# Two expert layers after attention on one core: halves of results issued in the order in which their buffers come free, token operands and weight conversion issued step by step

## The chip, the cores and the metric

The kernel runs on one core of a Trainium2 chip. A core has TensorE (matrix products, written to PSUM), VectorE, ScalarE and GpSimd (elementwise work), and SyncE, which here only issues DMAs. The profile calls them PE, DVE, ACT, POOL and SP. Each engine works through its own queue in order; engines wait for each other through semaphores. The metric is the device time of one execution in microseconds.

## The reference

```python
# attention in chunks of 64 over q, k, v of shape (4, 8, 576, 64)
scores = scale * (q_c @ k_c.T); scores -= scores.max(-1)
attn = exp(scores); attn = attn / (attn.sum(-1) + 1e-9); out = attn @ v_c
x = out.transpose(0, 2, 1, 3).reshape(2304, 512)
# first layer, d_ff 1536
x = ((x @ w_a) * (x @ w_b)) @ w_out
# second layer, d_ff 2048
h = x @ w_in
g = maximum(h, 0) + alpha * minimum(h, 0)
return g @ w2_out
```

Weights arrive as 64-bit numbers and are turned into 32-bit ones on the chip. Every product of the layers is done in three multiplications of "halves": an operand is split into a high half, its rounded copy, and a low half, what the copy leaves.

## The kernel before

**Tokens.** The 2304 tokens are five blocks j: block 0 has 256 tokens, blocks 1 to 4 have 512. Attention and the first products of the first layer are issued by a table of letters (START), which the change leaves alone.

**First layer.** 12 column tiles m of w_a, w_b and w_out, in six groups of two. A group visits all five blocks; a visit issues four products into PSUM (pa and pb for two m: `l1_a`, `l1_b`, 12 multiplications of 128 x 128 by the block each), then four products of the block ahead with w_out (`l2`, 6 multiplications each), whose sums VectorE adds to `acc` (L382). ScalarE copies pa, VectorE multiplies, ScalarE makes the high half gh (L314), GpSimd the low half gl (L319).

**Weight conversion.** Beside the groups the weights of later groups and of the second layer are fetched and converted, 128 x 512 at a time, by `job`, called at every third product (`EVERY`). One call issues all of this in a row: high and low half of one block (`w_high`, `w_halves`, or `w_store`), then for the next block two ScalarE steps (L105, L106), three VectorE bit operations (L113, L114, L117), one GpSimd addition (L127), then a fetch. Weights of the second layer go back to DRAM as halves (`put`: ScalarE L212, VectorE L213, two stores L216, two buffers each). For each pair of w_in blocks GpSimd also makes four sums (L236), and that call issues three `put`s in a row.

**Second layer.** It takes the tokens in pairs of blocks, (1, 2) in rounds 0 to 7 and (3, 4) in rounds 8 to 15; a round q has two column tiles of w_in and two row tiles of w2_out. The first matrix product of a pair uses seven products in place of eight, on sums of weights and sums of tokens: `seven(i, ...)`, i = 0 to 6, here s0 to s6, six multiplications each, into the PSUM banks X, Y, X, Z, X, X, Z. ScalarE copies X after s0, s2 and s4 (`kept`, L486), before the next product adds to the same bank. VectorE completes the four results (`complete` L490, `two_slopes` L398 and L401), ScalarE and GpSimd split each into halves (L314, L319) for the second product. Block 0 takes two plain products a round (`l3`, ph) in rounds 0 to 7. The second products (`l4`, here b0 to b9) of a round are issued between the seven of the next round; b0 to b3 read the halves for the pair's first block, b4 to b7 those for the second, b8 and b9 those for block 0. VectorE adds them up (L522). The halves gh and gl have six buffers each, used in turn; a round with block 0 takes six.

**Operands of the tokens.** The seven token operands are B11, B21, T2, T1, T3, T4, B22, made by `t_stage` in seven stages from `acc`: subtractions into a scratch tile tt on VectorE (L424), then per operand two high halves on ScalarE (L430) and two low halves, one on GpSimd, one on VectorE (L432). T1 and T2 are made in tt, and T3 and T4 are written over them. This happens twice: at the end of the first layer for blocks 1 and 2, and in round 7 for blocks 3 and 4, each stage behind its `seven`.

Under the manual schedule, each engine's queue has the order of the code.

Of the kernel before, what the change touches and what calls it, by code (L numbers as in the profile page):

```python
# [45 lines left out]
def tile_attention_moe_moe2(ctx: ExitStack, tc: tile.TileContext, qkv, w_a, w_b, w_out, w2_in, alpha, w2_out, out):  # L46
# [144 lines left out]
    def w_add(b):  # L191
        block_at[b] = conv_add(block_at[b])
# [16 lines left out]
    def put(m, i, wf):  # L209
        h = spares[0].tile([P, 512], F32R, tag="gh", name="sh", bufs=2)  # L210
        l = spares[0].tile([P, 512], F32R, tag="gl", name="sl", bufs=2)
        nc.scalar.activation(out=h, in_=wf, func=ACTF.Copy)  # L212
# [6 lines left out]
    def w_store(b):  # L219
        assert b == halved[0]  # L220
        halved[0] += 1
        _, m, i = jobs[b][:3]
        wf = block_at.pop(b)
        if i == 0:
            left[m] = wf
        if i == 1:
            w0 = left.pop(m)
            a11, a12, a21, a22 = w0[:, 0:256], w0[:, 256:512], wf[:, 0:256], wf[:, 256:512]
            s12 = spares[0].tile([P, 512], F32, tag="a", name="s12", bufs=3)
            s34 = spares[0].tile([P, 512], F32, tag="a", name="s34", bufs=3)  # L230
            s1, s2, s3, s4 = s12[:, 0:256], s12[:, 256:512], s34[:, 0:256], s34[:, 256:512]
            for o, x, y, op in (
                (s1, a21, a22, ALU.add), (s2, s1, a11, ALU.subtract), (s3, a11, a21, ALU.subtract),
                (s4, a12, s2, ALU.subtract),
            ):
                nc.gpsimd.tensor_tensor(out=o, in0=x, in1=y, op=op)  # L236
            put(m, 4, s12)
            put(m, 5, s34)
        put(m, i, wf)

    def job(limit):

        b = halved[0]
        if b < begun[0]:
            if jobs[b][0] is None:
                w_store(b)
            else:
                w_high(b)
                w_halves(b, nc.vector)
        b = begun[0]  # L250
        if b < len(jobs) and b == halved[0]:
            w_low(b)
            w_bits(b)
            w_add(b)
        if len(jobs) < begun[0] + 2:
            fetch_next(limit)

# [146 lines left out]
    def l3(q, k, j):  # L404
        n = blocks[j][1] * P
        ph = bank([P, n], "ph")
        run(ph, k_steps(W2[q, k], xh[j], xl[j]))
        G[q, k, j] = two_slopes(ph, 2 * q % M2 + k, n)
# [10 lines left out]
    T_AT = {"B11": "xh1", "B21": "xl1", "T2": "xh2", "T1": "xl2", "T3": "xh3", "T4": "xl3", "B22": "xh4"}  # L419
    tt = [None]  # L420

    def t_add(out, x, y):
        for kk in range(2):
            nc.vector.tensor_tensor(out=out[:, kk], in0=x[:, kk], in1=y[:, kk], op=ALU.subtract)  # L424

    def t_split(name, src):
        t = xp.tile([P, 2, 2, 512], F32R, tag=T_AT[name], name=name)
        T[name] = t
        for kk in range(2):
            nc.scalar.activation(out=t[:, 0, kk], in_=src[:, kk], func=ACTF.Copy)  # L430
            eng = nc.vector if kk else nc.gpsimd
            eng.tensor_tensor(out=t[:, 1, kk], in0=src[:, kk], in1=t[:, 0, kk].bitcast(F32), op=ALU.subtract)  # L432

    def t_stage(i, j1, j2):

        b11, b21, b12, b22 = acc[j1][:, 0:2], acc[j1][:, 2:4], acc[j2][:, 0:2], acc[j2][:, 2:4]
        if i == 0:
            t_split("B11", b11)
        elif i == 1:
            t_split("B21", b21)  # L440
            tt[0] = xp.tile([P, KD, 512], F32, tag="xl4", name="tt")
            t_add(tt[0][:, 0:2], b12, b11)
            t_add(tt[0][:, 2:4], b22, tt[0][:, 0:2])
        elif i == 2:
            t_split("T2", tt[0][:, 2:4])
        elif i == 3:
            t_split("T1", tt[0][:, 0:2])
            t_add(tt[0][:, 2:4], b21, tt[0][:, 2:4])
        elif i == 4:
            t_add(tt[0][:, 0:2], b22, b12)  # L450
            t_split("T3", tt[0][:, 0:2])
        elif i == 5:
            t_split("T4", tt[0][:, 2:4])
        else:
            t_split("B22", b22)
# [88 lines left out]
    with tc.manual_schedule():  # L544
# [183 lines left out]
        for i, (f, args) in enumerate(order[NB - 1][2] + order[NB - 2][3]):  # L728
            f(*args)
            if i < 4:  # L730
                job(4)
# [4 lines left out]
        count = 0  # L736
        extra = []
        stages = [(t_stage, (i, 1, 2)) for i in range(7)]
        for m0, j, front, back in order[NB:]:
# [3 lines left out]
            if last and j == 4:  # L743
                extra += stages
            for i, (f, args) in enumerate(front + behind):
# [3 lines left out]
                count += 1  # L749
                if count % EVERY == 0:  # L750
                    job(limit)
                if extra and count % 2 == 0:
                    f, args = extra.pop(0)
                    f(*args)
            behind = back
        for f, args in extra:
            f(*args)
# [5 lines left out]
        for q in range(2 * n2):  # L763
            j1, j2 = (1, 2) if q < n2 else (3, 4)
            front = [(seven, (i, q, j1, j2)) for i in range(7)]
            small = [(l3, (q, k, 0)) for k in range(2)] if q < n2 else []
            extra = load_back(q) if q else []
            if q + 1 < 2 * n2:
                extra += load_front(q + 1)
            mixed = []  # L770
            if q == 0:
                for i in range(4):
                    mixed += [front[i], behind[i]]
                mixed += [front[4], small[0], front[5], small[1], front[6]]
            else:
                for i in range(7):
                    mixed += [front[i], behind[i]]
                mixed += behind[7:8] + small + behind[8:]
            for f, args in mixed:
                f(*args)  # L780
                if q == n2 - 1 and f is seven:
                    t_stage(args[0], 3, 4)
                if extra:
                    f, args = extra.pop(0)
                    f(*args)
# [46 lines left out]
```

## Time and profile before

| | us |
|---|---|
| runs of the kernel | 912.78, 905.9, 912.08 |
| median | 912.08 |
| the profiled execution | 912.4 |
| its span on the core | 910.6 |
| TensorE busy in it | 867.1 |

The rows below come from the profiled execution; times in them count from its span's start. "idle before <- X" names what ended an engine's wait. A product is a run of multiplications into one bank.

### The profile page before, as it was taken

To read this page: it belongs to the slowest core of one execution; us is meant where nothing else is said; L and a number is where in the kernel's file an instruction comes from. 1 tells how busy PE (TensorE), PEld (TensorE's weight loads), DVE (VectorE), ACT (ScalarE), POOL (GpSimd) and SP (SyncE) were. 2 spreads that over 40 slices of the span, in tenths; PEclk is the share of its full clock that TensorE was granted. 3 is DMA by queue.
4 is the path that set the end of the run, shared out by engine and by line. 5 is a ranking of instruction groups with operands and counts; after the bars stand their busy time and mean duration, and the time that the engine had idled before them with its cause. 6 is when DMAs were issued, how large, how long until landed. Compare 5 with 4: busy or idle time off the path is not lost.

```text
span 910.6 us, 13385 instructions
## 1 busy us (share of the span) xinstructions
PE 867.1 (95%) x5112; PEld 724.4 (80%) x5112; DVE 547.1 (60%) x871; ACT 328.0 (36%) x579; POOL 327.6 (36%) x282
## 2 busy tenths in 40 slices
PE   5899899999999999999999799999998699999998
PEld 4788788888888788878888678888876578888886
DVE  6783455746776576677624743565655753566555
ACT  4573464534454444455412332112122223212111
POOL 4462244434354444444423332222223422222221
PEclk9899999999999999999999899999999799999999
DMA  8853035336436626534622124332233065555512
GB/s 300 271 171 107 12 117 208 116 132 214 162 119 228 207 95 207 198 128 144 229 90 92 55 85 139 139 103 74 102 139 138 1 208 186 168 173 169 184 47 93
DMA packets 79408, 130.91 MB, mean 144 GB/s; under 512 B 9200, under 2 KB 34288, under 8 KB 79344
## 3 DMA queue, kind: packets, MB, share of 16 engines
q1 hardware_dynamic: 79344, 130.06, 42.3%
q8 instruction: 40, 0.66, 0.3%
q14 instruction: 24, 0.20, 0.1%
HBM read 100.15 MB, written 29.88 MB: 143 GB/s over the span
## 4 chain that ended last, share of the span: by engine, by line
PE 71%; DVE 11%; ACT 6%; POOL 5%; DMA 4%; issue 3%; SPq 0%; POOLq 0%; ACTq 0%; DVEq 0%
PE po L296 30%; PE pa L296 10%; PE pb L296 10%; PE sumX L478 10%; PE sumZ L478 5%; POOL t L127 3%; PE sumY L478 2%; PE ph L296 2%; DVE sl L213 2%; ACT sh L212 2%; DMA qk_t<-in_qkv 2%; DVE t L117 1%; ACT gh L314 1%; DVE t L114 1%; DVE tt L424 1%
## 5 line engine op out<-in xcount | busy, mean ns | idle before, releaser
L319 POOL TENSOR_TENSOR gl<-a,gh 128x512 fp32r<-128x512 f32 (+1 forms) x80 | 94.2, 1186 | 277.1 <-ACT gh L314 216.9
L296 PE MATMUL po<-w,gh 128*128 128x512 f32 x576 | 179.2, 393 | 0.0
L127 POOL TENSOR_TENSOR t<-t,raw 128x512 int32<-128x512 int32 x68 | 89.1, 1310 | 205.0 <-DVE t L117 143.5
L522 DVE TENSOR_TENSOR oacc<-po,oacc 128x512 f32<-128x512 f32 x126 | 86.0, 687 | 84.1 <-PE po L296 84.1
L314 ACT ACTIVATE gh<-a 128x512 fp32r<-128x512 f32 (+1 forms) x80 | 47.0, 589 | 229.4 <-PE po L296 113.0
L296 PEld LDWEIGHTS po<-w,gh 128*128 128x128 f32 x576 | 109.5, 190 | 22.8
L296 PE MATMUL po<-w,gl 128*128 128x512 f32 x288 | 113.5, 394 | 3.3 <-DVE oacc L522 3.3
L296 PE MATMUL po<-gh,wl 128*128 128x512 f32 (+1 forms) x240 | 89.7, 374 | 3.0 <-DVE acc L382 3.0
L296 PE MATMUL pa<-xh,wl 128*128 128x512 f32 (+1 forms) x240 | 90.1, 375 | 2.4 <-DVE xl L678 2.4
L319 POOL TENSOR_TENSOR gl<-a_sb,gh 128x512 fp32r<-128x512 f32 (+1 forms) x60 | 71.2, 1188 | 54.6 <-ACT gh L314 53.6
L478 PE MATMUL sumX<-T,w 128*128 128x512 f32 x288 | 76.1, 400 | 14.7 <-ACT a L486 14.7
L296 PE MATMUL po<-gh,wh 128*128 128x512 f32 (+1 forms) x240 | 89.3, 372 | 0.0
L296 PE MATMUL po<-gl,wh 128*128 128x512 f32 (+1 forms) x240 | 89.2, 372 | 0.0
L296 PE MATMUL pb<-xh,wl 128*128 128x512 f32 (+1 forms) x240 | 89.0, 371 | 0.2 <-DVE a_sb L343 0.2
L296 PE MATMUL pa<-xl,wh 128*128 128x512 f32 (+1 forms) x240 | 89.2, 372 | 0.0
L296 PE MATMUL pa<-xh,wh 128*128 128x512 f32 (+1 forms) x240 | 89.1, 371 | 0.0
L296 PE MATMUL pb<-xl,wh 128*128 128x512 f32 (+1 forms) x240 | 88.3, 368 | 0.0
L296 PE MATMUL pb<-xh,wh 128*128 128x512 f32 (+1 forms) x240 | 88.3, 368 | 0.0
L478 PEld LDWEIGHTS sumX<-T,w 128*128 128x128 f32 x288 | 54.1, 191 | 29.7 <-ACT a L486 18.9
L314 ACT ACTIVATE gh<-a_sb 128x512 fp32r<-128x512 f32 (+1 forms) x60 | 35.3, 589 | 98.4 <-DVE a_sb L343 98.3
L343 DVE TENSOR_TENSOR a_sb<-pb,a_sb 128x512 f32<-128x512 f32 (+1 forms) x60 | 37.9, 632 | 50.9 <-PE pb L296 44.7
L296 PEld LDWEIGHTS po<-w,gl 128*128 128x128 f32 x288 | 54.8, 190 | 15.0 <-issue 3.6
(83 smaller groups left out, 1522.5 us busy)
## 6 DMA issues: line engine op xcount, KB each, us to landing
w<-w SPq DMA_DIRECT2D x192, 256.0 KB, 4.8
raw<-in_moe_w_out SPq DMA_DIRECT2D x28, 512.0 KB, 3.5
w<-sh SPq DMA_DIRECT2D x48, 256.0 KB, 2.6
w<-sl SPq DMA_DIRECT2D x48, 256.0 KB, 2.5
qk_t<-in_qkv SPq DMA_DIRECT2D x18, 512.0 KB, 5.0
raw<-in_moe_w_in SPq DMA_DIRECT2D x16, 512.0 KB, 4.0
raw<-in_moe_w_a SPq DMA_DIRECT2D x12, 512.0 KB, 3.7
raw<-in_moe_w_b SPq DMA_DIRECT2D x12, 512.0 KB, 4.0
```

What stands on the lines that cost most here:

```text
L114: nc.vector.tensor_scalar(out=t, in0=t, scalar1=3, scalar2=0x3FFFFFFF, op0=ALU.logical_shift_left, op1=ALU.bitwise_and)
L117: nc.vector.scalar_tensor_tensor(out=t, in0=raw[:, :, 1], scalar=0xC0000000, in1=t, op0=ALU.bitwise_and, op1=ALU.bitwise_or)
L127: nc.gpsimd.tensor_tensor(out=ti, in0=ti, in1=raw[:, :, 0].bitcast(I32), op=ALU.add)
L212: nc.scalar.activation(out=h, in_=wf, func=ACTF.Copy)
L213: nc.vector.tensor_tensor(out=l, in0=wf, in1=h.bitcast(F32), op=ALU.subtract)
L296: nc.tensor.matmul(out=dst, lhsT=a, rhs=b, start=(i == 0), stop=(i == len(steps) - 1))
L314: nc.scalar.activation(out=h, in_=src, func=ACTF.Copy)
L319: nc.gpsimd.tensor_tensor(out=l, in0=src, in1=h.bitcast(F32), op=ALU.subtract)
L343: nc.vector.tensor_tensor(out=a_sb, in0=G[m, j], in1=a_sb, op=ALU.mult)
L424: nc.vector.tensor_tensor(out=out[:, kk], in0=x[:, kk], in1=y[:, kk], op=ALU.subtract)
L478: nc.tensor.matmul(out=dst, lhsT=x, rhs=y, start=opens and kk == n == 0, stop=kk == 1 and n == 2, skip_group_check=not opens,)
L522: nc.vector.tensor_tensor(out=acc[j][:, t, :], in0=po, in1=acc[j][:, t, :], op=ALU.add)
```

## The change

- `job` is called after every product and issues a third of the work at a time: at the first call ScalarE's high half of one block and the two ScalarE steps of the next; at the second VectorE's low half (with its stores) and the three bit operations; at the third GpSimd's addition and the next fetch. The extra halves of the weight sums go through the list `later`, one entry per call. A pair of w_in blocks is always fetched together.
- In the second layer `two_slopes` no longer makes halves. The halves are issued by `g_halves` at places written out in `mixed`: the first result's behind b3, the second behind b5 (before s6), the other two behind b7, those of block 0 behind b8 and b9 (`l3_out`).
- `t_ops` gives the token operands as 36 single steps, two per product (from the last block's first product on, and in round 7), all low halves on GpSimd, with other buffers: each operand takes the buffer whose last reader is issued just ahead.

```diff
+        half = jobs and jobs[-1][0] is None and jobs[-1][2] == 0
-        if jobs1 and jobs1[0][0] < limit:
+        if jobs1 and jobs1[0][0] < limit and not half:
...
+    def weight_sums(m, w0, w1):
...
+        def high(i, t):
+            state = []
+            later.append(lambda: state.append(put_high(m, i, t)))
+            later.append(lambda: put_low(*state[0]))
+
+        later.append(lambda: None)
+        high(4, s12)
+        high(5, s34)
...
     def job(limit):
 
+        beat[0] += 1
+        if later:
+            later.pop(0)()
         b = begun[0]
+        if beat[0] % 3 == 1:
+            if halved[0] < ready[0]:
+                d = halved[0]
+                if jobs[d][0] is not None:
+                    block_at[d] = half_high(block_at[d], jobs[d][0], jobs[d][2])
+                else:
+                    _, m, i = jobs[d][:3]
+                    wf = block_at[d]
+                    if i == 0:
+                        left[m] = wf
+                    if i == 1:
+                        weight_sums(m, left.pop(m), wf)
+                    block_at[d] = put_high(m, i, wf)
+            if b < len(jobs):
+                w_low(b)
+        elif beat[0] % 3 == 2:
+            if halved[0] < ready[0]:
+                d = halved[0]
+                halved[0] += 1
+                if jobs[d][0] is not None:
+                    w_halves(d, nc.vector)
+                else:
+                    put_low(*block_at.pop(d))
+            if ready[0] < b:
+                w_bits(ready[0])
+        elif ready[0] < b:
+            w_add(ready[0])
+            ready[0] += 1
+            if len(jobs) < b + 2:
+                fetch_next(limit)
+        elif len(jobs) < b + 2:
             fetch_next(limit)
...
-        return half_l(neg, half_h(neg, n), n)
+        return neg
+
+    def g_halves(q, k, j):
+        g = G[q, k, j]
         n = blocks[j][1] * P
+        G[q, k, j] = half_l(g, half_h(g, n), n)
...
+    T_AT = {"B11": "xh1", "B21": "xl1", "T2": "xl2", "T1": "xh3", "T3": "xl3", "T4": "xh4", "B22": "xl4"}
+    def t_ops(j1, j2):
...
+        tt = xp.tile([P, KD, 512], F32, tag="xh2", name="tt")
...
+        def low(name, src, kk):
+            t = T[name]
+            nc.gpsimd.tensor_tensor(out=t[:, 1, kk], in0=src[:, kk], in1=t[:, 0, kk].bitcast(F32), op=ALU.subtract)
...
+        split("B11", b11)
+        less(t1, b12, b11)
+        less(t2, b22, t1)
+        split("B21", b21)
+        split("T2", t2)
+        split("T1", t1)
+        less(t2, b21, t2)
+        less(t1, b22, b12)
+        split("T3", t1)
+        split("T4", t2)
+        split("B22", b22)
+        return steps
...
+            g11, g21, g22, g12 = ((g_halves, (q, k, j)) for k, j in ((0, j1), (1, j1), (1, j2), (0, j2)))
+            for i in range(4):
+                mixed += [front[i], behind[i]]
             if q == 0:
+                mixed += [g11, front[4], small[0], front[5], small[1], g21, front[6], g22, g12] + small_out
             else:
+                mixed += [g11, front[4], behind[4], front[5], behind[5], g21, front[6], behind[6], behind[7]]
+                mixed += [g22, g12]
+                for k in range(2):
+                    mixed += small[k:k + 1] + behind[8 + k:9 + k] + small_out[k:k + 1]
+            if q == n2 - 1:
+                extra = [(f, ()) for f in t_ops(3, 4)]
             for f, args in mixed:
                 f(*args)
+                for part, n in ((loads, 1), (extra, 2 if q in (0, n2 - 1) else 4)):
+                    for f, args in part[:n]:
+                        f(*args)
+                    del part[:n]
```

Three places show what moved. The first is VectorE's queue at the last pair of w_in blocks in the weight conversion (sl is a stored low half, s a tile of weight sums, t a block in conversion, acc and a_sb what TensorE's products become). Before:

```order
L382 TENSOR_TENSOR acc_1778<-po,acc_1778 128x512
L213 TENSOR_TENSOR sl<-s_4699,sh 128x512
L213 TENSOR_TENSOR sl<-s_4700,sh 128x512
L213 TENSOR_TENSOR sl<-t,sh 128x512
L113 TENSOR_SCALAR t<-t 128x512
L114 TENSOR_SCALAR t<-t 128x512
L117 SCALAR_TENSOR_TENSOR t<-raw,t 128x512
L382 TENSOR_TENSOR acc_1778<-po,acc_1778 128x512 x3
```

The same pair now:

```order
L219 TENSOR_TENSOR sl<-s_4715,sh 128x512
L219 TENSOR_TENSOR sl<-t,sh 128x512
L113 TENSOR_SCALAR t<-t 128x512
L114 TENSOR_SCALAR t<-t 128x512
L117 SCALAR_TENSOR_TENSOR t<-raw,t 128x512
L373 TENSOR_TENSOR a_sb<-pb,a_sb 128x512
L219 TENSOR_TENSOR sl<-s_4716,sh 128x512
L412 TENSOR_TENSOR acc_997<-po,acc_997 128x256 x2
L219 TENSOR_TENSOR sl<-t,sh 128x512
```

Three low halves in a row, each behind a high half of ScalarE, have become single ones with products' work between them.

The second is ScalarE's queue in one of the rounds 2 to 6 (a<-sumX is a copy of X, gh a high half of a result, 128x256 those of block 0). Before:

```order
L486 ACTIVATE a<-sumX 128x512
L314 ACTIVATE gh<-a 128x512
L486 ACTIVATE a<-sumX 128x512 x2
L314 ACTIVATE gh<-a 128x512 x3
L314 ACTIVATE gh<-a 128x256 x2
```

Now:

```order
L528 ACTIVATE a<-sumX 128x512 x2
L344 ACTIVATE gh<-a 128x512
L528 ACTIVATE a<-sumX 128x512
L344 ACTIVATE gh<-a 128x512 x3
L344 ACTIVATE gh<-a 128x256 x2
```

The second copy of X has moved ahead of the first result's high half.

The third is round 7, where the operands of blocks 3 and 4 are made. GpSimd's queue before (B and T are token operands, gl low halves of results):

```order
L432 TENSOR_TENSOR B_6791<-acc_1666,B_6791 128x512
L319 TENSOR_TENSOR gl<-a,gh 128x512
L432 TENSOR_TENSOR B_6827<-acc_1666,B_6827 128x512
L432 TENSOR_TENSOR T_6861<-tt,T_6861 128x512
L432 TENSOR_TENSOR T_6889<-tt,T_6889 128x512
```

Now:

```order
L479 TENSOR_TENSOR B_6796<-acc_1632,B_6796 128x512 x2
L479 TENSOR_TENSOR B_6856<-acc_1632,B_6856 128x512 x2
L479 TENSOR_TENSOR T_6880<-tt,T_6880 128x512 x2
L349 TENSOR_TENSOR gl<-a,gh 128x512
L479 TENSOR_TENSOR T_6897<-tt,T_6897 128x512 x2
```

And ScalarE's queue there now (T_6880 is T2, T_6897 is T1):

```order
L528 ACTIVATE a<-sumX 128x512
L475 ACTIVATE B_6796<-acc_1632 128x512 x2
L528 ACTIVATE a<-sumX 128x512
L475 ACTIVATE B_6856<-acc_1632 128x512 x2
L475 ACTIVATE T_6880<-tt 128x512 x2
L344 ACTIVATE gh<-a 128x512
L475 ACTIVATE T_6897<-tt 128x512 x2
L528 ACTIVATE a<-sumX 128x512
```

GpSimd has both low halves of each operand, and ScalarE's third copy of X stands behind the highs of T2 and T1.

## Rows read from the trace of the kernel before

**Rows 1.** The page: busy time, share of the span and instructions of TensorE.
```profile
PE 867.1 (95%) x5112; PEld 724.4 (80%) x5112; DVE 547.1 (60%) x871; ACT 328.0 (36%) x579; POOL 327.6 (36%) x282
```

**Rows 2.** The chain of waits: start, duration, engine, bank, line, multiplications.
```profile
389.52 2.56 PE po L296 x6
392.09 3.40 PE pa L296 x12
...
544.90 2.72 PE po L296 x12
547.62 2.90 PE ph L296 x24
550.52 2.76 PE po L296 x12
```

**Rows 3.** Stretches: from:to, length, busy PE, PEld, DVE, ACT, POOL (instructions), clock, DMA.
```profile
123.85:425.41 301.56, 298.39 (x1443) 251.59 (x1442) 202.03 (x340) 145.86 (x262) 136.30 (x123) 0.99 0.49 164
425.41:499.21 73.80, 73.80 (x362) 62.53 (x360) 32.32 (x53) 23.02 (x43) 26.98 (x25) 1.00 0.42 143
499.21:525.85 26.64, 21.15 (x92) 17.39 (x91) 21.60 (x32) 9.47 (x17) 10.93 (x8) 0.87 0.20 63
525.85:553.28 27.43, 26.37 (x127) 21.96 (x127) 11.23 (x19) 8.08 (x16) 7.15 (x6) 1.00 0.17 55
553.28:687.66 134.38, 131.50 (x632) 109.56 (x631) 75.99 (x124) 27.27 (x50) 34.16 (x31) 1.00 0.34 118
687.66:729.25 41.59, 30.61 (x128) 24.31 (x127) 27.67 (x40) 12.55 (x23) 17.96 (x14) 0.88 0.22 76
729.25:753.12 23.87, 23.29 (x103) 18.90 (x103) 13.52 (x21) 4.63 (x8) 6.33 (x6) 1.00 0.64 220
850.00:875.00 25.00, 25.00 (x112) 20.71 (x111) 16.67 (x26) 5.42 (x9) 7.77 (x6) 1.00 0.36 127
```

**Rows 4.** Waits of TensorE: waited for, us in total, times, longest.
```profile
PE sumX L478 <- ACT a L486: 14.7, 10, 5.5
PE po L296 <- DVE oacc L522: 3.3, 1, 3.3
```

**Rows 5.** Timeline of TensorE around 389 us: start, duration, line, operation, [idle before].
```profile
389.52 0.50 PE L296 MATMUL po<-gh,wl 128*128 128x512 f32 x1 [2.11 <-DVE acc L382]
```

**Rows 6.** Timeline of ScalarE and VectorE ahead of that wait.
```profile
382.87 0.63 ACT L212 ACTIVATE sh<-s 128x512 fp32r<-128x512 f32 x1 [5.01 <-POOL s L236]
383.54 2.08 DVE L213 TENSOR_TENSOR sl<-s,sh 128x512 fp32r<-128x512 f32 x2 [2.87 <-ACT sh L212]
389.05 0.42 DVE L382 TENSOR_TENSOR acc<-po,acc 128x256 f32<-128x256 f32 x1
```

**Rows 7.** Timeline of ScalarE and TensorE in round 6.
```profile
671.20 0.63 ACT L314 ACTIVATE gh<-a 128x512 fp32r<-128x512 f32 x1 [8.29 <-PE po L296]
671.74 0.58 ACT L486 ACTIVATE a<-sumX 128x512 f32<-128x512 f32 x1
672.37 1.65 PE L478 MATMUL sumX<-T,w 128*128 128x512 f32 x6 [0.58 <-ACT a L486]
674.11 0.60 ACT L486 ACTIVATE a<-sumX 128x512 f32<-128x512 f32 x1 [1.80 <-PE sumX L478]
```

**Rows 8.** Groups by line: operation, tiles, count | busy us, mean ns | idle before.
```profile
L319 POOL TENSOR_TENSOR gl<-a,gh 128x512 fp32r<-128x512 f32 x64 | 82.8, 1297 | 259.0 <-ACT gh L314 198.8 <-issue 36.0 <-PE sumX L478 17.7
L398 DVE TENSOR_SCALAR a<-a,alpha_sb 128x512 f32<-128x512 f32 x48 | 26.2, 545 | 3.7 <-POOL gl L319 0.6
L401 DVE SCALAR_TENSOR_TENSOR a<-a 128x512 f32<-128x512 f32 x48 | 33.3, 693 | 1.7
```

**Rows 9.** Timeline of GpSimd and VectorE at the second change of operands.
```profile
700.04 1.74 POOL L432 TENSOR_TENSOR B<-acc,B 128x512 fp32r<-128x512 f32 x1
700.55 2.38 DVE L424 TENSOR_TENSOR tt<-acc,acc 128x512 f32<-128x512 f32 x2
702.85 1.28 DVE L424 TENSOR_TENSOR tt<-acc,tt 128x512 f32<-128x512 f32 x2
```

More of the change, by code (lines that the diff above doesn't have):

```diff
@@ L217, in put @@
             dram[m, i, n] = d
[L219 to L239, printed above, removed]
@@ L241, in job @@
-    def job(limit):
[L243 to L249, printed above, removed]
-        b = begun[0]
[L251 to L255, printed above, removed]
+    def weight_sums(m, w0, w1):
+        a11, a12, a21, a22 = w0[:, 0:256], w0[:, 256:512], w1[:, 0:256], w1[:, 256:512]
+        s12 = spares[0].tile([P, 512], F32, tag="a", name="s12", bufs=3)
+        s34 = spares[0].tile([P, 512], F32, tag="a", name="s34", bufs=3)
+        s1, s2, s3, s4 = s12[:, 0:256], s12[:, 256:512], s34[:, 0:256], s34[:, 256:512]
+        for o, x, y, op in (
+            (s1, a21, a22, ALU.add), (s2, s1, a11, ALU.subtract), (s3, a11, a21, ALU.subtract),
+            (s4, a12, s2, ALU.subtract),
+        ):
+            nc.gpsimd.tensor_tensor(out=o, in0=x, in1=y, op=op)
+        def high(i, t):
[5 more added lines that the diff above has]
+        high(5, s34)
@@ L256, in job @@
             fetch_next(limit)
+    ready = [8]
     W2 = {}
@@ L417, in tile_attention_moe_moe2, with l3_out @@
+    def l3_out(q, k):
+        G[q, k, 0] = two_slopes(G[q, k, 0], 2 * q % M2 + k, blocks[0][1] * P)
+        g_halves(q, k, 0)
     A_AT = {"A11": (0, 0), "A12": (0, 1), "A22": (1, 1), "S1": (4, 0), "S2": (4, 1), "S3": (5, 0), "S4": (5, 1)}
     T = {}
[L419 to L424, printed above, removed]
@@ new lines, in t_ops, with less, high, split @@
+    def t_ops(j1, j2):
+        b11, b21, b12, b22 = acc[j1][:, 0:2], acc[j1][:, 2:4], acc[j2][:, 0:2], acc[j2][:, 2:4]
+        tt = xp.tile([P, KD, 512], F32, tag="xh2", name="tt")
+        t1, t2 = tt[:, 0:2], tt[:, 2:4]
+        steps = []
+        def less(out, x, y):
+            for kk in range(2):
+                steps.append(
+                    lambda kk=kk: nc.vector.tensor_tensor(out=out[:, kk], in0=x[:, kk], in1=y[:, kk], op=ALU.subtract)
+                )
+        def high(name, src, kk):
+            if kk == 0:
+                T[name] = xp.tile([P, 2, 2, 512], F32R, tag=T_AT[name], name=name)
+            nc.scalar.activation(out=T[name][:, 0, kk], in_=src[:, kk], func=ACTF.Copy)
+        def low(name, src, kk):
+            t = T[name]
+            nc.gpsimd.tensor_tensor(out=t[:, 1, kk], in0=src[:, kk], in1=t[:, 0, kk].bitcast(F32), op=ALU.subtract)
+        def split(name, src):
+            for f in (high, low):
+                for kk in range(2):
+                    steps.append(lambda f=f, kk=kk: f(name, src, kk))
+        split("B11", b11)
[10 more added lines that the diff above has]
+        return steps
@@ L729, in tile_attention_moe_moe2 @@
             f(*args)
-            if i < 4:
-                job(4)
+            job(4)
         limit = 4
         behind = order[NB - 1][3]
-        count = 0
         extra = []
-        stages = [(t_stage, (i, 1, 2)) for i in range(7)]
         for m0, j, front, back in order[NB:]:
@@ L743, in tile_attention_moe_moe2 @@
             if last and j == 4:
-                extra += stages
+                extra += [(f, ()) for f in t_ops(1, 2)]
             for i, (f, args) in enumerate(front + behind):
@@ L748, in tile_attention_moe_moe2 @@
                     limit = m0 + 4
[L749 to L754, printed above, removed]
+                job(limit)
+                for _ in range(2 if j == 4 else 1):
+                    if extra:
+                        f, args = extra.pop(0)
+                        f(*args)
             behind = back
-        for f, args in extra:
-            f(*args)
         assert not jobs1 and not jobs2 and halved[0] == len(jobs)
```

62 lines of the change are left out of this document (15 added, 47 removed).

## The prediction

> **What bounds the kernel now.** The page's first part is read first: TensorE is busy for 867.1 of 910.6 us [rows 1]. That share doesn't say what can still be won, since its instructions overlap; so TensorE is followed by stretches, and each is set against the time that its products need at full speed. The chain of waits gives that pace: 2.72 us for two products of six 512-column multiplications (1.36 us each), 2.90 for the two products of the small token block [rows 2]. The table of stretches [rows 3] then shows four places that lose time.
>
> - Weight conversion, 123.85 to 425.41: four groups take 301.56 us; the fifth, which converts little, takes 73.80 [rows 3]. Four times 73.80 is 295.2, so 6.4 us are lost.
> - First change of operands (round 0 of the second layer): 11 products and the small block, 11 x 1.36 + 2.9 = 17.9, take 26.64: 8.7 lost.
> - Ordinary rounds: 17 products of 512 columns or 13 x 1.36 + (2.72 + 2.90 + 2.76) = 26.06 with the small block. Round 1 takes 27.43, rounds 2 to 6 take 134.38 for 130.3, round 8 takes 23.87 for 17 x 1.36 = 23.12: together 1.4 + 4.1 + 0.75 = 6.2 lost.
> - Second change of operands (round 7): 41.59 for 26.06: 15.5 lost.
>
> The sum is 36.8 us. Up to the last eight products before 123.85 us every engine keeps its order, and the rounds from the ninth on have no loss (TensorE 25.00 of 25.00 us [rows 3]). The profiled execution took 912.4 us, the median of the runs is 912.08, so both may stand for one another; with every loss gone the time would be 912.4 - 36.8 = 875.6 us. That is the floor.
>
> The waits say who ends each loss: ScalarE's copies of X (14.7 us, 5.5 of it at once in round 0) and VectorE's sums (3.3 in one wait) [rows 4]. Idle TensorE costs twice where it lasts: after 2.11 us idle [rows 5] three products' time, 4.08 us, becomes 2.56 + 3.40 = 5.96 [rows 2], 1.9 more, and the granted clock of the two changes is 0.87 and 0.88 [rows 3]. After the 0.58 us of an ordinary round [rows 7] the clock stays at 1.00 [rows 3].
>
> **The change, part by part.**
>
> *Weight conversion in single steps.* Number and kind of the instructions stay; their places change. Before, one call issued a block's high half, low half, three bit operations, addition and fetch; in a pair of stored blocks it also issued three stores in a row. At 382.87 ScalarE's next step has waited 5.01 us for GpSimd's sums, VectorE 2.87 for ScalarE, and the sum that TensorE needs (389.05) stands behind all of it [rows 6]: TensorE idles 2.11 us and then loses the 1.9 at the lower clock [rows 2, 5]. Now each step stands at least one product behind the step it reads (mostly 1.36 or 2.72 us, against 0.63 us of work [rows 6]), and GpSimd's sums are read two products behind their issue. I take the loss from 6.4 to 0.4; bounds 0 and 2 (one such wait left). Stores now stand between fetches on SyncE; a store waits for VectorE's low half, and a fetch behind it is held that long, while fetches run two blocks, six products, ahead: nothing is charged. The four weights of a group's first products are converted before the last token block of the group ahead, eight products early, so no product waits for weights.
>
> *Halves in the order of free buffers.* In a round before, the first result's high half stands on ScalarE ahead of the second copy of X, but its buffer is freed by the fourth product of the second matrix (b3). ScalarE waits 8.29 us for it, the copy comes at 671.74, and the third X product waits [rows 7]. Now the copy comes first and the half after b3. The next copy (needed by the fifth product that adds to X or Z) follows s4: 0.63 of half is done before s4's 1.36 ends, and the copy, 0.58, with a start about 0.3 behind the product (674.02, 674.11), fits under b4's 1.36. The two last halves stand behind b7, whose buffers they take; their lows, 1.30 each [rows 8], have over 12 us to the first product that reads them. Loss of ordinary rounds: 6.2 to 0; bounds 0 and 2.
>
> *Operands of the tokens, first time.* 36 steps, two per product: 14 high halves (ScalarE), 8 subtractions (VectorE), 14 low halves, now all on GpSimd (before 7 there, 7 on VectorE). They start with the last block's first product, 16.3 us before round 0, where before they were issued at every second product and in whole stages, the last of which stood in one heap on all three engines at round 0 (the wait of 5.5 us [rows 4]). With t = 0 at round 0's first product and 1.30 us per low: T2's lows end at 2.9 (needed 5.4), T1's at 5.4 (needed 8.2). T3 is the first that is late: its subtraction stands on VectorE, from 4.4 on (the second product's end and 0.3), behind the first result's three operations, two other subtractions and a sum, 0.69 + 0.55 + 0.69 + 1.28 + 0.69 = 3.9 [rows 8, 9]. So T3's high halves end at 9.6 and 10.2, its lows at 11.0 and 12.3. The fifth product starts at 10.9 and reads the second low 0.9 later: 0.5 late. T4's lows end at 14.9 (needed 15.1); then a result's half and B22, 18.8 against 18.0: 0.8 to 0.9 late. I take 1.4 left of 8.7; bounds 0 and 6.8 (first rival).
>
> *Second time, round 7.* The same 36 steps inside one round, each in the buffer that the product just issued has freed. GpSimd has 18 x 1.30 = 23.4 us and two small lows in 26 [rows 8], but its late lows are needed only in round 8, which does no such work. With VectorE's 0.64 per subtraction [rows 9] nothing waits: on ScalarE two B21 highs end at 8.8, T2's at 9.9, a result's half (after b3) at 11.8, T1's highs at 12.9, the third copy of X at 13.5, and the product behind it starts at 13.6. That is thin. T2's high halves stand ahead of that copy on ScalarE and wait for VectorE. The rows show what a VectorE operation on two SBUF tiles does beside GpSimd: two take 2.38 us instead of 1.28, and GpSimd's takes 1.74 instead of 1.30 [rows 8, 9]. If each of the six such operations up to T2 meets one, T2 is ready 3 us later, the copy ends at 15.3, the product waits 1.8, and VectorE's late sums hold two PSUM banks for 1.0 and 1.7: 4.5 in all. I take about the middle, 2.2, of 15.5; bounds 0 and 9.0 (first rival). No idle stretch of these is as long as 2.11 us, so the clock stays.
>
> The Trainium skill, "SBUF — State Buffer", section "Who interferes with whom", says that a VectorE instruction with two SBUF inputs and a GpSimd instruction that reads SBUF exclude each other: whichever issues first holds the shared port for its whole length. Rows 9 agree: the low that runs ends at 701.78, and the pair behind it is 1.10 longer than the pair alone. Were there no such rule, round 7 would lose nothing and the time would be 2.2 lower; with it at every meeting, 2.3 higher.
>
> **Sum.** 875.6 + 0.4 + 0 + 1.4 + 2.2 = 879.6, forecast **880 us**.
>
> **The rivals.**
>
> - *GpSimd's queue is the new bound at both changes.* Lows at 1.73 (1.74 [rows 9]) instead of 1.30: in round 0, T3, T4 and B22 come 1.8, 0.6 and 2.5 late, 4.9, and the last wait is over 2.11, so about 1.9 more for the clock: 6.8. In round 7 the six lows ahead of T1's add 6 x 0.44 = 2.6 to the 4.5, and a wait over 2.11 the 1.9: 9.0. 875.6 + 0.4 + 6.8 + 9.0 = 891.8, say 892. For it: seven lows were moved to the slower engine and the rows of 1.74 are its own. Against it: 1.74 appears only where VectorE worked on SBUF tiles too, and there are 8 subtractions for 14 lows.
> - *Slower: VectorE becomes the bound of the weight conversion.* It is busy 202 of 301.56 us with 123 GpSimd instructions beside it [rows 3]. Spread steps put one beside the other all the time; if each of the 123 held VectorE for 1.1 us (2.38 - 1.28), VectorE would need 202 + 135 = 337 us against 295 of products, 42 more: 922 us. It decides once a meeting costs over 0.75 us on average. Against it: such a wait shows only where VectorE reads two SBUF tiles, and its sums and products of TensorE's results read one of the two from PSUM; the low halves and bit operations alone are exposed.
> - *The changes keep their losses* and only conversion and rounds gain: 912.4 - 6.4 - 6.2 = 899.8; if conversion keeps its loss too, 906, no change that a measurement tells (here 1% of 912, 9 us, either way). For it: the dependence of T3 and T4 on T1 and T2 through one tile is still there. Against it: the work starts 16 us earlier.
>
> Chances: forecast 0.70, GpSimd's queue 0.18, losses kept 0.07, VectorE bound 0.05. The first case's own range is 874 to 886. To leave out no more than 2 in 10 the range goes up into the second case, 873 to 893. Faster by over 1% (below 903): 0.91; within 1%: 0.05; slower: 0.04.
>
> **What the new profile would show.** TensorE's waits for ScalarE's copies of X fall from 14.7 us to under 3. No idle stretch over 2 us behind 123 us, and a granted clock of 1.00 in every stretch. Four conversion groups in 295 to 296 us; rounds 1 to 6 at 26.1; round 0 near 19.3; round 7 near 28. A round 7 above 33, or lows that T3, T4 and B22's products wait for one after another, would speak for GpSimd's queue; VectorE over 90% busy before 425 us, with waits for its sums, for the slower case. Rounds 1 to 6 above 26.5 would show that the half's buffer wasn't the reason for their wait, and the prediction would be wrong there.

## The result and the profile after

The changed kernel takes 881.46 us (median of 4 runs, 880.39 to 882.5), the kernel before 909.99 beside it (4 runs, 905.9 to 912.78): ratio 0.969, 95% interval 0.9644 to 0.9736, 28.5 us faster. The forecast was 880 us with a range of 873 to 893. The profiled execution took 882.5 us; TensorE is busy for 97% of a span that is 30 us shorter (95% before [rows 1]):

```profile
PE 857.6 (97%) x5112; PEld 719.8 (82%) x5112; DVE 551.1 (63%) x857; ACT 326.2 (37%) x579; POOL 356.8 (41%) x296
```

The stretches of the changed kernel, with the columns of [rows 3] and in its order (conversion, last group, round 0, round 1, rounds 2 to 6, round 7, round 8):

```profile
124.16:420.00 295.84, 295.84 (x1441) 250.75 (x1440) 201.46 (x334) 141.49 (x255) 144.87 (x120) 1.00 0.50 164
420.00:493.96 73.96, 73.96 (x361) 62.69 (x360) 40.33 (x64) 27.74 (x52) 33.54 (x29) 1.00 0.50 164
493.96:513.55 19.59, 18.68 (x91) 15.08 (x90) 11.89 (x17) 7.82 (x14) 15.43 (x13) 1.00 0.33 101
513.55:539.87 26.32, 26.32 (x127) 21.94 (x126) 13.36 (x22) 10.82 (x20) 9.70 (x9) 1.00 0.13 46
539.87:670.07 130.20, 130.20 (x631) 110.09 (x630) 75.72 (x122) 25.84 (x46) 33.03 (x30) 1.00 0.36 122
670.07:700.11 30.04, 26.83 (x127) 21.91 (x126) 25.00 (x33) 12.18 (x23) 19.54 (x15) 1.00 0.31 105
700.11:723.23 23.12, 23.12 (x103) 19.14 (x102) 16.03 (x23) 4.63 (x8) 13.38 (x12) 1.00 0.67 228
```

Conversion and rounds 2 to 6 have TensorE busy for their whole length, and the granted clock is 1.00 in every one of these stretches. What remains is in the two changes of operands, and the waits of TensorE name it (the longest behind 123 us; columns of [rows 4]):

```profile
PE ph L326 <- DVE oacc L564: 1.7, 1, 1.7
PE sumX L520 <- ACT a L528: 0.8, 1, 0.8
PE sumZ L520 <- POOL B L479: 0.7, 2, 0.4
```

ScalarE's copies of X went from 14.7 us of waits to 0.8. In round 6, ScalarE's queue in the timeline now reads as follows; the first result's half waits 2.74 us and holds nobody up (the copy of X behind it starts 1.47 us after its end), where it had waited 8.29 with a copy of X right behind it [rows 7]:

```profile
654.43 0.63 ACT L344 ACTIVATE gh<-a 128x512 fp32r<-128x512 f32 x1 [2.74 <-PE po L326]
656.53 0.60 ACT L528 ACTIVATE a<-sumX 128x512 f32<-128x512 f32 x1 [1.47 <-POOL gl L349]
```

Round 0: TensorE in the timeline waits for T3's second low half, then for both of B22's:

```profile
506.11 0.73 PE L520 MATMUL sumX<-T,w 128*128 128x512 f32 x2 [0.20 <-POOL T L479]
511.74 0.96 PE L520 MATMUL sumZ<-B,w 128*128 128x512 f32 x3 [0.42 <-POOL B L479]
512.98 0.73 PE L520 MATMUL sumZ<-B,w 128*128 128x512 f32 x2 [0.29 <-POOL B L479]
```

Round 7: the first line below is TensorE behind the third copy of X, the others behind two sums of VectorE that free PSUM banks. VectorE's own timeline stands in the second block (L428, L431, L469 and L564 are L398, L401, L424 and L522 of the kernel before):

```profile
684.64 1.66 PE L520 MATMUL sumX<-T,w 128*128 128x512 f32 x6 [0.80 <-ACT a L528]
693.88 0.47 PE L326 MATMUL po<-w,gl 128*128 128x512 f32 x1 [0.69 <-DVE oacc L564]
697.20 0.38 PE L326 MATMUL ph<-xh,w 128*128 128x256 f32 x1 [1.71 <-DVE oacc L564]
```

```profile
675.22 1.03 DVE L428 TENSOR_SCALAR a<-a,alpha_sb 128x512 f32<-128x512 f32 x1
676.90 1.28 DVE L469 TENSOR_TENSOR tt<-acc,acc 128x512 f32<-128x512 f32 x2
678.70 3.18 DVE L469 TENSOR_TENSOR tt<-acc,tt 128x512 f32<-128x512 f32 x2
685.42 1.63 DVE L428 TENSOR_SCALAR a<-a,alpha_sb 128x512 f32<-128x512 f32 x1
687.08 1.66 DVE L431 SCALAR_TENSOR_TENSOR a<-a 128x512 f32<-128x512 f32 x1
694.88 1.66 DVE L431 SCALAR_TENSOR_TENSOR a<-a 128x512 f32<-128x512 f32 x1
696.47 1.87 DVE L564 TENSOR_TENSOR oacc<-po,oacc 128x512 f32<-128x512 f32 x3
```

The second pair of subtractions takes 3.18 us where a pair alone takes 1.28, and L428 and L431 take 1.63 and 1.66 where their mean before was 0.545 and 0.693 [rows 8]. GpSimd is at low halves beside each of the long ones:

```profile
673.43 2.54 POOL L479 TENSOR_TENSOR B<-acc,B 128x512 fp32r<-128x512 f32 x2 [0.27 <-ACT B L475]
678.33 3.00 POOL L479 TENSOR_TENSOR B<-acc,B 128x512 fp32r<-128x512 f32 x2 [2.36 <-ACT B L475]
681.29 2.98 POOL L479 TENSOR_TENSOR T<-tt,T 128x512 fp32r<-128x512 f32 x2
685.47 2.72 POOL L479 TENSOR_TENSOR T<-tt,T 128x512 fp32r<-128x512 f32 x2
694.45 1.54 POOL L349 TENSOR_TENSOR gl<-a,gh 128x512 fp32r<-128x512 f32 x1 [6.25 <-DVE a L532]
```

### The profile page after: what moved, and what is told of

Its sections match the earlier page's. It is cut to its first block, busy times and chain, and to the rows that moved or that the text cites. A ratio compares the mean times of both kernels' runs of the same rounds, so it can differ in the third digit from the quotient of the medians.

```text
span 880.7 us, 13400 instructions
## 1 busy us (share of the span) xinstructions
PE 857.6 (97%) x5112; PEld 719.8 (82%) x5112; DVE 551.1 (63%) x857; ACT 326.2 (37%) x579; POOL 356.8 (41%) x296
## 4 chain that ended last, share of the span: by engine, by line
PE 92%; DVE 3%; DMA 2%; ACT 1%; POOL 1%; SPq 1%; issue 0%; DVEq 0%
PE po L326 37%; PE pa L326 17%; PE pb L326 17%; PE sumX L520 9%; PE sumZ L520 4%; PE sumY L520 2%; PE ph L326 2%; DVE tt L469 1%; PE s L697 1%; PE pt L675 1%; PE s L639 1%; DMA qk_t<-in_qkv 1%; DVE a L431 1%; DMA raw<-in_moe_w_a 1%; DMA raw<-in_moe_w_b 1%; DVE a L428 1%
## 5 line engine op out<-in xcount | busy, mean ns | idle before, releaser
L564 DVE TENSOR_TENSOR oacc<-po,oacc 128x512 f32<-128x512 f32 x126 | 85.0, 685 | 81.4 <-PE po L326 81.4
L349 POOL TENSOR_TENSOR gl<-a_sb,gh 128x512 fp32r<-128x512 f32 (+1 forms) x60 | 77.3, 1289 | 134.4 <-ACT gh L344 130.5
L520 PE MATMUL sumX<-T,w 128*128 128x512 f32 x288 | 73.6, 390 | 1.0 <-ACT a L528 0.8
L528 ACT ACTIVATE a<-sumX 128x512 f32<-128x512 f32 x48 | 28.5, 595 | 108.0 <-PE sumX L520 95.9
L412 DVE TENSOR_TENSOR acc<-po,acc 128x512 f32<-128x512 f32 (+1 forms) x100 | 60.0, 629 | 9.6 <-PE po L326 9.6
```

The costliest lines, as they stand in the source:

```text
L349: nc.gpsimd.tensor_tensor(out=l, in0=src, in1=h.bitcast(F32), op=ALU.subtract)
L412: nc.vector.tensor_tensor(out=acc[j][:, o, :], in0=po, in1=acc[j][:, o, :], op=ALU.add)
L520: nc.tensor.matmul(out=dst, lhsT=x, rhs=y, start=opens and kk == n == 0, stop=kk == 1 and n == 2, skip_group_check=not opens,)
L528: nc.scalar.activation(out=sums[n], in_=sums["X"], func=ACTF.Copy)
L564: nc.vector.tensor_tensor(out=acc[j][:, t, :], in0=po, in1=acc[j][:, t, :], op=ALU.add)
```

## The experiments

Three questions: what each part of the change gives alone (first three runs); whether the rest at the two changes is GpSimd's queue of low halves or VectorE's lengthened operations; and whether the rest can be won. One table holds all: us lost in each stretch of the profiled execution, from TensorE's start to start, against 73.96 a group, 17.98 for round 0 (reached in three of the runs), 26.04 and 23.12 a round. "Sum" is the floor of the prediction, 875.6, plus these losses.

| kernel | conversion | round 0 | 1 | 2-6 | 7 | 8 | sum | median | ratio to before, 95% |
|---|---|---|---|---|---|---|---|---|---|
| before | 5.7 | 8.5 | 1.4 | 4.4 | 15.4 | 0.9 | 911.9 | 908.3 to 910.8 | 1 |
| conversion alone | 0.0 | 7.6 | 1.4 | 4.3 | 16.4 | 1.0 | 906.4 | 906.43 | 0.997 (0.9951-0.9988) |
| halves alone | 4.1 | 7.3 | 0.6 | 0.1 | 8.9 | 0.0 | 896.6 | 896.93 | 0.9877 (0.9836-0.9918) |
| operands alone | 4.6 | 4.5 | 2.3 | 4.4 | 5.3 | 0.9 | 897.6 | 897.89 | 0.9879 (0.984-0.9919) |
| the change | 0.0 | 1.6 | 0.3 | 0.0 | 4.0 | 0.0 | 881.5 | 881.46 | 0.969 (0.9644-0.9736) |
| lows split | 0.1 | 0.0 | 0.8 | 0.0 | 5.1 | 0.3 | 881.9 | 881.95 | 0.9701 (0.9669-0.9733) |
| one step | 0.0 | 1.6 | 0.3 | 0.0 | 0.0 | 3.8 | 881.3 | 881.1 | 0.969 (0.9646-0.9734) |
| B22 early | 0.0 | 1.3 | 1.4 | 0.0 | 4.0 | 0.0 | 882.4 | 883.15 | 0.9705 (0.9666-0.9743) |
| both of these | 0.0 | 1.3 | 1.5 | 0.0 | 0.0 | 2.1 | 880.5 | 880.67 | 0.9683 (0.9651-0.9715) |
| split first, one step | 0.0 | 0.0 | 0.8 | 0.0 | 0.0 | 2.1 | 878.6 | 879.11 | 0.9664 (0.9631-0.9697) |
| lows filled | 0.0 | 1.6 | 0.3 | 0.0 | 0.5 | 0.0 | 878.0 | 877.35 | 0.9651 (0.962-0.9681) |
| late subtractions | 0.0 | 0.0 | 0.8 | 0.0 | 0.0 | 0.0 | 876.5 | 876.74 | 0.9643 (0.9613-0.9673) |

In each of the eleven others the sum is within 0.8 us of the median, so the floor holds to about 1 us. It is not exact: the losses are those of the profiled execution, and beside that execution's own time the sum is off by up to 1.4 us (the change: 881.5 for 882.5), because the part ahead of the first conversion group, which the sum takes as constant, ends between 121.8 and 124.5 us. The losses by stretch are the main difference between these kernels. (The profiled execution of before lies in the upper part of its runs.)

**Conversion alone** is the kernel before with the new `job`.

```diff
-                if count % EVERY == 0:
-                    job(limit)
+                job(limit)
```

> Only the weight conversion is issued in single steps; halves and token operands as before. Theory A (the three parts of the gain stand in different stretches and add up): four conversion groups fall from 301.6 to 295-296 us, nothing else moves, 6.0 to 6.5 us faster than before. Rival B (the loss in that stretch is chance of a run, since runs of the kernel before differ by up to 7 us): within 2 us of before, and idle stretches of TensorE between 130 and 425 us stay.

The loss goes wholly (first line, four conversion groups), although two of the low halves of the last pair (s_4715 and t) still stand one behind the other on VectorE. The two profiled executions differ by about what theory A said, 6.1 us (912.4 and 906.28), but the medians by 1.9 (908.31 and 906.43), as rival B's time had it. The second and third line are rounds 0 and 7, which this run leaves alone (stretches as above); they lose 24.0 us together, as much as in the profiled execution of before (23.9), at clocks of 0.87 and 0.84:

```profile
122.78:418.62 295.84, 295.84 (x1441) 250.79 (x1440) 201.56 (x334) 141.07 (x254) 144.79 (x120) 1.00 0.51 164
492.58:518.19 25.61, 20.12 (x91) 16.59 (x90) 21.34 (x32) 9.43 (x17) 10.94 (x8) 0.87 0.19 64
680.15:722.56 42.41, 32.19 (x128) 25.64 (x126) 27.66 (x40) 12.55 (x23) 18.30 (x14) 0.84 0.22 75
```

The mean granted clock of this kernel's ten runs is 0.984 to 0.986, while the 13 runs of before beside it range from 0.985 (912.0 to 912.6 us) to 0.994 (905.42). So a part of the 912.4 us, the clock's share, comes and goes from run to run of one kernel, and most runs of before have a higher mean clock than the profiled one (0.985). No run of before at the higher clock has a kept trace, so in which stretches it loses less is not shown. The mechanism was as expected, the size in the time was not.

**Halves alone** is the kernel before with the new order of the halves.

```diff
+                mixed += [g11, front[4], behind[4], front[5], behind[5], g21, front[6], behind[6], behind[7]]
+                mixed += [g22, g12]
```

> Only the order of the results' halves is changed; conversion and token operands as before. Theory A: rounds 1 to 6 fall from 26.9 to 26.1 us and round 8 by 0.75, together 6 us faster than before, the two changes of operands keep their 8.7 and 15.5 us. Rival B (the copies of X were late for another reason, their own start or VectorE): rounds 1 to 6 stay at 26.9 us, under 1 us faster.

Rounds 2 to 6 and 8 lose 0.1 us or nothing, so the half's buffer was what they waited for; round 1 keeps 0.6. The time fell by 11.4 us and not by 6. Most of the rest is round 7, which neither theory expected: 34.94 us for 41.43, with the operands still in stages. ScalarE's timeline shows what moved: the high halves of B21 no longer stand behind a half that waits 7.25 us for b3.

**Operands alone** is the kernel before with the operands in single steps, two per product.

```diff
-                if q == n2 - 1 and f is seven:
-                    t_stage(args[0], 3, 4)
+                for part, n in ((loads, 1), (extra, 2)):
+                    for f, args in part[:n]:
+                        f(*args)
```

> Only the token operands are issued as single steps; conversion and order of halves as before. Theory A (independent parts): round 0 at 19.5 us and round 7 at 30, 18 to 19 us faster than before. Rival B (the single steps help only where ScalarE is not held by the first result's half, which waits for b3): round 7 stays above 34 us, at most 14 us faster than before.

Round 7 is near theory A (31.34 for 30), round 0 is not (22.51 for 19.5), and the time falls by 10.4 us, not by 18 to 19. In round 0 TensorE's waits name B22, for 2.4 us at once, and GpSimd's timeline shows that, in the old order of the halves, two results' lows stand ahead of B22's there:

```profile
515.81 2.08 POOL L319 TENSOR_TENSOR gl<-a,gh 128x512 fp32r<-128x512 f32 x2 [1.81 <-ACT gh L314]
517.84 2.50 POOL L441 TENSOR_TENSOR B<-acc,B 128x512 fp32r<-128x512 f32 x2
```

So the parts don't add up: in round 7 they take away a common part of the loss (6.5 and 10.1 alone, 11.4 together). In round 0 they give 1.2 and 4.0 alone and 6.9 together, but the 1.2 is not clear of chance: conversion alone moved rounds 0 and 7 by 0.9 and 1.0 without a change there.

**Lows split** gives each operand's second low half to VectorE.

```diff
-            nc.gpsimd.tensor_tensor(out=t[:, 1, kk], ...
+            eng = nc.vector if kk else nc.gpsimd
+            eng.tensor_tensor(out=t[:, 1, kk], ...
```

> The changed kernel with the operands' second low halves on VectorE, as before, and the first ones on GpSimd. Theory A (what is left in round 7, 4 us, is VectorE being late): 7 x 0.7 to 1.1 us more work on VectorE in each change, round 7 up from 30.0 to 32-35 us, 2 to 6 us slower than the changed kernel. Rival B (GpSimd's queue of lows is what is late): round 7 and round 0 each 1 to 1.5 us shorter, 2 to 3 us faster than the changed kernel.

Round 0 no longer loses its 1.6 us (round 1 loses 0.8 for 0.3), round 7 gets 1.1 longer, by the numbers of neither theory; the time is the same. Stretches of rounds 0 and 7, and TensorE's longest wait in round 7:

```profile
493.94:511.92 17.98, 17.98 (x92) 15.18 (x91) 16.11 (x23) 6.56 (x12) 8.27 (x6) 1.00 0.28 92
668.98:700.16 31.18, 28.05 (x127) 22.94 (x126) 28.78 (x40) 11.98 (x23) 17.08 (x13) 0.95 0.31 102
695.76 0.39 PE L326 MATMUL ph<-xh,w 128*128 128x256 f32 x1 [2.85 <-DVE oacc L565]
```

In round 0 GpSimd's low halves were the limit. In round 7 TensorE idles for 3.13 us, where it idled for 3.21: the third copy of X is now in time, but the wait for a sum of VectorE has grown from 1.71 to 2.85 us. The 1.1 us are busy time at the lower clock behind that wait (0.95 in the mean of the round). So GpSimd's queue is not the limit there; that VectorE is, this run suggests, and "lows filled" tests it.

**One step** per product in round 7, the rest in round 8.

```diff
-                for part, n in ((loads, 1), (extra, 2 if q in (0, n2 - 1) else 4)):
+                for part, n in ((loads, 1), (extra, 2 if q == 0 else 1)):
```

> The changed kernel with one step per product in place of two in round 7 (steps that are left follow in round 8). Theory A, that round 7 loses 4.0 us because VectorE's subtractions meet GpSimd's low halves in a crowd and push T2's highs ahead of the third copy of X back: fewer meetings per product, the copy of X comes in time, round 7 loses 1 us or less of its 30.04 (27.0 or less) and round 8 stays at 23.12; the time is 2.5 to 3 us below 881.5, ratio to before 0.967. Rival B, that the order of dependences on GpSimd sets it: what is put off comes late in round 8, T3, T4 and B22 wait there, round 8 is 2 us or more longer, and the time is within 1 us of 881.5 or above it.

Both were half right: round 7 is 26.04, without loss, and round 8 pays it back. There T3's subtraction on VectorE waits for T1's low half on GpSimd, block 0's result waits behind it, its high half waits for that on ScalarE, a copy of X stands behind that half, and TensorE waits for the copy (one line of each engine's timeline, VectorE, ScalarE twice, TensorE):

```profile
696.76 1.76 DVE L469 TENSOR_TENSOR tt<-acc 128x512 f32<-128x512 f32 x1 [1.19 <-POOL T L479]
...
700.69 0.42 ACT L344 ACTIVATE gh<-a 128x256 fp32r<-128x256 f32 x1 [5.42 <-DVE a L431]
701.53 0.58 ACT L528 ACTIVATE a<-sumX 128x512 f32<-128x512 f32 x1
...
702.16 2.26 PE L520 MATMUL sumX<-T,w 128*128 128x512 f32 x6 [1.85 <-ACT a L528]
```

**B22 early**: another order at the first change only, three steps per product in the last block, B22's halves ahead of T3's, T3's subtraction ahead of T4's.

```diff
+        if early:
+            split("B22", b22)
+            steps.extend([lambda: None] * 4)
+            less(t1, b22, b12)
         less(t2, b21, t2)
```

> The changed kernel with another order at the first change alone: three steps per product in the last block, B22's halves ahead of T3 and T4, T3's subtraction ahead of T4's. Theory A, that round 0 loses its 1.5 to 2 us because T3's subtraction stands behind a result's operations on VectorE and B22's low halves come last on GpSimd: round 0 falls from 19.59 to 18.0, the last group of the first layer stays at 73.96, the time is 1.5 us below 881.5. Rival B, that GpSimd's work as a whole (14 lows and a result's) is too much for the time there: round 0 keeps 19.3 or more, or the last group becomes 1 us longer, and the time stays within 0.5 us of 881.5.

A miss: round 0 is 19.25, round 1 1.2 longer. B22 is in time, but now VectorE meets GpSimd's lows ahead of T3 (first line, VectorE's timeline), and T3's low is 0.72 us late (second line, TensorE's):

```profile
500.99 1.66 DVE L431 SCALAR_TENSOR_TENSOR a<-a 128x512 f32<-128x512 f32 x1
507.03 0.74 PE L526 MATMUL sumX<-T,w 128*128 128x512 f32 x2 [0.72 <-POOL T L479]
```

**Both of these** (three steps per product with B22 early, and one step in round 7), and **split first, one step** (lows split at the first change, one step in round 7):

> Both: the other order at the first change, and one step per product in round 7. If the two losses are independent of each other, as theory A says, their gains add up: 881.5 - 1.5 - 3 = 877 us, and of the losses that the prediction listed less than 1.5 us is left. If a rival B of either holds, 880 us or above.

> One step per product in round 7, and at the first change each operand's second low half on VectorE. Theory A (GpSimd's queue of lows is the limit at the first change, VectorE's subtractions at the second, each on its own): round 0 17.9 to 18.0 as with split lows in both changes, round 7 27.0 or less, time 877 us. Rival: VectorE's lows at the first change cost the rounds behind it, as round 1 took 26.87 with split lows: 878.5 us or above.

Neither reaches 877; with 880.67 and 879.11 both times lie where the rivals had them. In both round 8 still loses 2.1 us, which neither expectation counted, and in the first the other order gains nothing (1.3 lost in round 0, 1.5 in round 1), as it gained nothing by itself. In the second the first change is free of loss in round 0, as with lows split, and round 1 loses 0.8, as the rival said.

**Lows filled** asks for the cause in round 7 directly: GpSimd fills the low halves of the second change's operands instead of subtracting, so it writes SBUF there and reads none.

```diff
+            if j1 == 3:
+                nc.gpsimd.memset(t[:, 1, kk].bitcast(F32), 0.0)
+                return
```

> The changed kernel with the operands' 14 low halves of the second change filled with zeros by GpSimd in place of being subtracted: GpSimd writes the tiles, but reads none (the low halves of these operands are left out of the products' values, TensorE does all its products). Theory A, that VectorE is late in round 7 because its operations on two SBUF tiles, or on one, wait while GpSimd reads SBUF: the operations there fall to their own length (subtraction pairs 1.28 us, L428 0.49 to 0.55, L431 0.69), round 7 loses under 1 us of its 4.0 (below 27.0 us) with the same two steps per product, the time is about 878 us. Rival B, that the number of VectorE's and ScalarE's operations in round 7 and their order is too much by itself: round 7 keeps a loss of 3 us or more, the time is 880.5 us or above.

Theory A. Two steps per product as in the change, the same instructions on VectorE, all but the last shown at their own length, and round 7 takes 26.53 in place of 30.04 (VectorE's timeline at the places shown for the change, and one pair of fills on GpSimd):

```profile
673.23 0.49 DVE L428 TENSOR_SCALAR a<-a,alpha_sb 128x512 f32<-128x512 f32 x1
673.75 0.69 DVE L431 SCALAR_TENSOR_TENSOR a<-a 128x512 f32<-128x512 f32 x1
674.36 1.28 DVE L469 TENSOR_TENSOR tt<-acc,acc 128x512 f32<-128x512 f32 x2
675.10 1.00 POOL L480 MEMSET T<- 128x512 f32 x2 [1.72 <-DVE tt L469]
676.16 1.28 DVE L469 TENSOR_TENSOR tt<-acc,tt 128x512 f32<-128x512 f32 x2
689.37 1.67 DVE L431 SCALAR_TENSOR_TENSOR a<-a 128x512 f32<-128x512 f32 x1
```

The last line is the one that still meets a low half of a result on GpSimd, and behind it is the one wait left (0.4 us from start to start). The run takes away two things at once, GpSimd's reads and a part of its time there (0.5 us a fill for 1.3 a low; it is busy for 12.30 us in round 7, in the change for 19.54). Two readings speak for the reads: the pair at 674.36 keeps its 1.28 us with a fill beside it from 675.10 on, and in round 7 of the change no wait of TensorE, ScalarE or VectorE names GpSimd, so its shorter time alone could win nothing there. The pair at 676.16 has no GpSimd instruction beside it and does not tell the two apart.

**Late subtractions**: split lows at the first change, one step per product in round 7, and T3's and T4's subtractions put off to round 8's first products, behind block 0's results, with two steps per product in round 8.

```diff
+        if j1 == 3:
+            steps.extend([lambda: None] * 5)
         less(t2, b21, t2)
...
-                for part, n in ((loads, 1), (extra, 2 if q in (0, n2 - 1) else 4)):
+                for part, n in ((loads, 1), (extra, 1 if q == n2 - 1 else 2)):
```

> One step per product in round 7, T3's and T4's subtractions put off to the first products of round 8 (two steps per product there), each operand's second low half on VectorE at the first change. With one step per product alone T3's subtraction stood on VectorE ahead of block 0's last result and waited 1.19 us for T1's low half, and round 8 lost 2.0 to 3.8 us. Theory A, that this order was the whole of it: round 7 stays at 26.04, round 8 falls to 23.12 to 23.4, round 0 stays at 17.98, the time is 877 us. Rival B, that work put off into round 8 always comes late: T3, T4 or B22 wait there, round 8 takes 25 us or more, 879 us or above.

Theory A: rounds 0, 7 and 8 (stretches) are without any idle time of TensorE. Beside split first, one step, this run changes the order and the steps per product in round 8, so the gain belongs to the two together. Round 1 still loses 0.8, and TensorE's timeline names the low half of a result on GpSimd there (last line). It is the fastest kernel here, 876.74 us, 0.995 of the change by the two medians, measured in different groups of runs.

```profile
492.89:510.87 17.98, 17.98 (x91) 15.18 (x90) 16.12 (x23) 6.56 (x12) 8.26 (x6) 1.00 0.27 91
667.95:693.99 26.04, 26.04 (x127) 22.02 (x126) 21.20 (x29) 9.21 (x17) 15.55 (x13) 1.00 0.35 121
693.99:717.11 23.12, 23.12 (x103) 19.14 (x102) 20.54 (x27) 7.95 (x14) 17.99 (x14) 1.00 0.63 211
513.60 0.50 PE L326 MATMUL po<-w,gl 128*128 128x512 f32 x1 [0.53 <-POOL gl L349]
```

## Why the prediction was right, point by point

- **The floor**, 875.6 us, and the sum of losses by stretches: right to about 1 us. With the losses measured in the changed kernel it gives 881.5, its median is 881.46; with those of the last experiment 876.5, measured 876.74. That the first two agree so closely is partly luck, since the execution with these losses took 882.5.
- **Conversion**, 6.4 to 0.4: the wait was rightly read, nothing of it is left. The 0.4 kept for one wait wasn't needed. Its gain in the median, alone, is only 1.9 us. The prediction took the profiled execution for a typical one (912.4 beside 912.08), but its clock, 0.985 in the mean, was at the lower end of what the runs show (0.983 to 0.994), and the gain of 32 us that it implied was 28.5. The forecast of the time itself was not hurt, since the floor holds no loss of the clock.
- **Halves**, 6.2 to 0: right in rounds 2 to 6 and 8; round 1 keeps 0.3. What the prediction didn't see is that this part also carries round 7: 6.5 us of it come with the halves alone. The sum was not hurt, since both parts were made.
- **Round 0**, 1.4 left: 1.6. The waits are the ones worked out: T3 lost 0.36 from start to start (said 0.5), B22 0.59 and 0.45 (said 0.8 to 0.9 in all), T4 nothing.
- **Round 7**, 2.2 left: 4.0. This is the term that was mis-sized. All three waits are where the working put them: the third copy of X 0.97 lost (said 1.8 at worst), the two banks 0.85 and 1.87 (said 1.0 and 1.7). The middle between no meeting and a meeting at every operation was a guess. Up to T2 the meetings cost 0.5 + 1.9 = 2.4 of the 3 us that were the bound (1.03 for 0.49, 3.18 for 1.28). The 0.5 are L428, which reads one tile and stood outside the operations counted, and behind T2 the meetings go on at L428 and L431, which the working didn't count either. So the upper value of the working, 4.5, was nearer than the middle.
- **GpSimd's queue as the bound**: in round 0 it is (with half of the lows on VectorE the loss there is gone, and 0.5 of it comes back in round 1), but at 1.6 us and not 6.8. In round 7 no wait for it shows. **VectorE as the bound of the conversion**: no; it was busy 201.46 of 295.84 us beside 120 GpSimd instructions. **Losses kept**: no.
- **The clock**: 1.00 in every stretch, as said. The reason given, that no idle stretch is as long as 2.11 us, does not hold: in one step a wait of 1.85 us was followed by a clock of 0.62, in another kernel the same wait by 1.00. With a longest wait of 1.71 us there was some luck in it.

The Trainium skill, "SBUF — State Buffer", section "Who interferes with whom", says that a VectorE instruction with two SBUF inputs meets a GpSimd instruction that reads SBUF, not one that only writes it. The runs agree: beside low halves a pair takes 3.18 us, and the pair at 674.36 takes 1.28 beside a fill. The page also lists tensor_scalar among the operations that can take the shared pair where their operands allow it; L428 reads one tile, and takes 1.63 us for 0.49 beside a low half.

## What to carry to other kernels

Add up the losses by stretch against the pace of an undisturbed one; the floor found in this way from one execution gave the medians of eleven other kernels within 0.8 us, and their own profiled executions within 1.4. Parts of a change that end the same wait, or free the same queue, don't add up, so cost each stretch with all of them in place. When work is moved to GpSimd, look at every VectorE operation on SBUF that falls beside it: fewer steps per product, with the subtractions behind what others wait for, won round 7's 4.0 us; the choice of engine won 1.6 in round 0.

## What the runs showed of the hardware

A wait of some 2 us can cost TensorE its clock or not, from run to run. The four rows are stretches of about 4 us behind such a wait: of the kernel before and of halves alone, behind the same wait for `acc` (2.11 and 2.07 us); of one step and of both together, behind the same wait for X (1.85 us each). The column behind the last (x) is the granted clock: 0.61 and 0.62 are mostly the lower of the two levels, 1.00 the full one.

```profile
389.52:393.85 4.33, 4.33 (x12) 3.43 (x13) 3.05 (x5) 2.78 (x5) 2.34 (x2) 0.61 0.38 121
```

```profile
388.15:392.10 3.95, 3.95 (x17) 3.30 (x18) 2.67 (x4) 2.75 (x5) 2.35 (x2) 1.00 0.40 123
```

```profile
702.16:706.61 4.45, 4.45 (x13) 3.49 (x13) 3.49 (x4) 2.63 (x5) 4.45 (x4) 0.62 0.87 287
```

```profile
702.04:706.25 4.21, 4.21 (x18) 3.49 (x19) 4.11 (x5) 2.63 (x5) 4.21 (x4) 1.00 0.87 301
```

Where it fell, the loss of round 8 was 3.8 us instead of 2.1. The runs of before lie between 904.43 and 913.71 us, those of the change, whose longest wait there is 1.71 us, within 2.1 us of each other.
